# Asking for three z sets and two filter sets in five successive steps

## The chip, the cores and the metric

The kernel runs on one core of one Trainium2 chip. The metric is the device time of one execution in microseconds (us); times below are the median of several executions, and a profile shows one execution.

## The reference

Two blocks follow each other. The first mixes along the sequence with a filter in the frequency domain, the second is a feed-forward layer with a hard-swish:

```
x (8, 3008, 256);  filt_r, filt_i (1505, 256)
X = rfft(x, axis=1);  Y = X * (filt_r + 1j*filt_i);  y = irfft(Y, n=3008, axis=1)
h = y.reshape(24064, 256) @ w_in            # w_in (256, 2048)
g = h * clip(h + 3, 0, 6) / 6
out = g @ w_out                             # w_out (2048, 256)
```

Everything is float32.

## The kernel before

**The transform.** The 3008-point transform of a batch is split as 64 x 47. Its first stage (`a6_unit`, `a6_sums`, L486 to L516) reads x, and GpSimd's queue stores its result as "z" in the DRAM tensor `z_tmp` (`z6_store`, L517). The second stage reads z back, multiplies with 64-point tables on TensorE (`b_unit`, L549), multiplies with the filter on VectorE (`f_unit`, L583 and L584; `y_unit` adds), and transforms back (`bi3_unit`). Its result goes to `g_tmp` in DRAM, from where `t4_load` (L717) fetches it for the last stage (`n_five`, `n_unit`), whose products are the tokens' features `xn`.

**Sets.** A batch's second stage has 12 units, and two units share one z set and one filter set, so there are `NT` = 6 of each per batch, 512 KB apiece. `t2_load(n, c)` (L543) fetches z set c of batch n into one of `TB` = 3 buffers `t2`; `table_load(n, c)` (L257 for batches 2 to 7) fetches filter set c from `f_tmp` into one of `FB` = 2 buffers `ft`. `b_unit(n, 2c)` needs z set c; `f_unit(n, 2c)` needs filter set c.

**The feed-forward layer.** The 24064 tokens are 47 blocks of 512, held as 256 pairs. A block has `NP` = 8 steps, one for each 256 columns of `w_in`; a step takes some 5.6 us when nothing of the transform is in it. The layer uses a Strassen-like scheme with seven products for eight. `up_1` to `up_5` make h in two PSUM tiles `al` and `be`; VectorE adds corrections to them (L835 reads `be`, L840 reads `al`), ScalarE makes the clipped factor (L854), VectorE multiplies (L859). `down` multiplies the result of the step before with `w_out` into four PSUM tiles `po`. `out_1` to `out_5` collect a finished block, and `store` (L988) writes it: one DMA of 256 KB to the DRAM tensor `o_tmp` (L990), seven to ten DMAs of up to 47 rows of 1 KB straight into the output (L993), and, in some blocks, one DMA from `o_tmp` into the output (L998, 423 to 752 KB), for the rows that are mirrored in the sequence.

**Order.** The order of the work is written out by hand. `at(step, fn, ...)` puts a piece of the transform into a step of the feed-forward layer, and a step runs its pieces in places: 3 and 4 at its head (with a `b_unit` and its `f_unit` beside an `n_five`), 0 and 1 in its middle, 2 at its end. All loads are in place 2. Each engine works through its own instructions in that order. All loads and stores named here but `z6_store` and `g3_store` are issued on SyncE's queue, which works in order too.

With k the first step of batch n's tokens, the last piece of the first stage stands in step k-41. The five steps that matter here are called +0 (step k-40) to +4 (step k-36). In the kernel before, +0 ends with five loads. Step +1 is the second step of a block and holds the `store` of the block before (at `out_5`, ahead of place 2). Step +2 has, in places 3 and 4, `n_five`, `b_unit(n, 0)` and `f_unit(n, 0)`. Step +3 has `t4_load` and `f_unit(n, 1)` at its end, and step +6 `b_unit(n, 2)` and `f_unit(n, 2)`. In step +2 the last product into `al` (`up_5`, called A22 below) comes after L840's reading of `al`, which comes after `f_unit(n, 0)` on VectorE.

Of the kernel before, what the change touches and what calls it, by code (L numbers as in the profile page):

```python
# [44 lines left out]
TB = 3  # L45
FB = 2
# [130 lines left out]
def kernel(  # L177
# [498 lines left out]
    for b in range(B):  # L676
# [4 lines left out]
        n = 0  # L681
# [336 lines left out]
    def at(step, fn, *a):  # L1018
        plan.setdefault((step, 0 if fn in EARLY else 1 if fn in (w_scale, bi3_unit, a6_unit) else 2), []).append((fn, a))

    with tc.manual_schedule():
# [175 lines left out]
        def places(n):  # L1197
            if n == 1:
                return (list(range(2, NB + 2)), [12, 13, 14, 18, 19, 20, 22, 23, 26, 27, 29, 31],
                        [13, 15, 16, 19, 21, 22, 24, 25, 28, 30, 30, 32], [17, 24, 30, 34])  # L1200
            k = first[n] * NP
            a_at = [k - 7 * NP + i for i in A_AT]
            f_at, y_at, bi_at = ([k - (5 - 2 * r) * NP + i for r in range(2) for i in p]
                                 for p in ((2, 3, 6, 7, 12, 13), (4, 5, 10, 11, 14, 15), (11, 16)))
            return a_at, f_at, y_at, bi_at
# [4 lines left out]
        for n in range(1, B):  # L1210
            a_at, f_at, y_at, bi_at = places(n)
            for c, s in enumerate(a_at):
                at(s, a_unit if n == 1 else a6_unit, n, c)
                at(s, a_sums if n == 1 else a6_sums, n, c)
                at(s, *((z_store, n, c, nc.sync) if n == 1 else (z6_store, n, c)))
                if c >= (3 if n == 1 else 2):
                    at(max(a_at[c - 3 + (n > 1)], s - 6), x_load, n, c)
                elif n > 1:
                    at(max(prev[-1 if n == 2 else c - 2], s - 6), x_load, n, c)
            for c in range(NT):  # L1220
                s = f_at[2 * (c - TB) + (n == 1)] + 1 if c >= TB else a_at[-1] + 1
                at(s, t2_load, n, c)
                s = f_at[2 * (c - FB) + 1] + 1 if c >= FB else a_at[-1] + 1
                at(s, table_load, n, c)
                if n == 1:
                    at(f_at[2 * c], table_store, c)
            for i in range(NU):
                if (f_at[i], 3) in plan and n > 1:
                    plan[f_at[i], 3].append((b_unit, (n, i)))
                elif i % 2 == 0 or n == 1:  # L1230
                    at(f_at[i], b_unit, n, i)
                if i % 3 == 0:
                    at(bi_at[i // 3], bi3_unit, n, i)
                    at(bi_at[i // 3], g3_store, n, i)
                at(y_at[i], y_unit, n, i)
            for i in range(NU):
                if (f_at[i], 3) in plan and n > 1:
                    plan.setdefault((f_at[i], 4), []).append((f_unit, (n, i)))
                else:
                    at(f_at[i], f_unit, n, i)  # L1240
            prev = a_at
# [122 lines left out]
```

## Time and profile before

| | |
|---|---|
| median of three executions | 2613.17 us (2611.69 to 2617.41) |
| the profiled execution | 2615.35 us, of which the span is 2613.5 |
| TensorE busy | 2588.2 us of the span (99%) |
| VectorE busy | 1894.6 us (72%) |
| ScalarE busy | 1298.1 us (50%) |
| GpSimd busy | 444.1 us (17%) |
| mean granted TensorE clock | 0.997 |
| z set loads (L543) | 42 of 512 KB |
| filter set loads (L257) | 36 of 512 KB |

The span runs from the first to the last instruction that the profile shows. Busy times of different engines overlap. A line "idle ... <-X" names what ended an engine's idle time. For SyncE the profile shows when it issues a DMA and how long the issue takes; when a DMA has landed is taken from the completion marks that the trace keeps for each.

### The profile page before, as it was taken

Reading aid. Unit: us, or ns where it says so; the run is one execution under the profiler, and the core shown is the slowest. Engines: PE = TensorE matmul, PEld = TensorE weight load, DVE = VectorE, ACT = ScalarE, POOL = GpSimd, SP = SyncE. Lnnn points to the kernel's source line nnn. Section 1 sums busy time; section 2 is a strip of 40 time slices with the busy share of each in tenths; the row PEclk is TensorE's granted clock in tenths of the full one; section 3 lists DMA queues with packets and bytes.
Section 4 is the critical chain, followed back from the end, with each engine's and each line's share of the span. In section 5 each row is a group of like instructions: output and inputs, shape, how many; then the busy total and the mean of one; then the engine's idle time right before and its main releaser. Section 6 shows DMA issues by size and latency. Waiting matters only on the chain.

```text
span 2613.5 us, 87737 instructions
## 1 busy us (share of the span) xinstructions
PE 2588.2 (99%) x38466; PEld 2071.5 (79%) x38466; DVE 1894.6 (72%) x3526; ACT 1298.1 (50%) x2682; POOL 444.1 (17%) x671
## 2 busy tenths in 40 slices
PE   8999999999999999999999999999999999999998
PEld 4588877888788887888878888778877888888886
DVE  7877777777777776777777777767776777767665
ACT  4554454545545455454554445545455454555554
POOL 3251031101311012110121101211102111011110
PEclk9999999999999999999999999999999999999999
DMA  9734233222332222321223222232122321111000
GB/s 241 212 110 117 70 103 101 57 57 63 88 106 67 57 61 80 114 63 55 65 73 114 65 61 58 74 111 64 54 61 79 114 64 35 49 44 25 18 22 25
DMA packets 119141, 202.51 MB, mean 77 GB/s; under 512 B 17522, under 2 KB 85712, under 8 KB 118374
## 3 DMA queue, kind: packets, MB, share of 16 engines
q1 hardware_dynamic: 105261, 148.30, 19.9%
q0 software_dynamic: 13216, 48.35, 7.0%
q8 instruction: 302, 4.95, 0.8%
q14 instruction: 81, 0.66, 0.1%
q10 hardware_dynamic: 281, 0.24, 0.0%
HBM read 121.42 MB, written 87.13 MB: 80 GB/s over the span
## 4 chain that ended last, share of the span: by engine, by line
PE 98%; DMA 0%; issue 0%; ACT 0%; DVE 0%; SPq 0%; POOL 0%; POOLq 0%; ACTq 0%
PE po L806 45%; PE al L806 25%; PE be L806 19%; PE psf L565 1%; PE psf L498 1%; PE psn L746 1%; PE al L746 1%; PE psf L640 1%; PE be L640 1%; PE be L498 1%; PE psf L573 0%; DMA g_tmp<-t 0%; PE psf L471 0%; PE psn L806 0%; PE be L746 0%
## 5 line engine op out<-in xcount | busy, mean ns | idle before, releaser
L806 PEld LDWEIGHTS po<-w_all,g 128*64 128x64 f32 x20808 | 1248.0, 137 | 229.0 <-issue 12.7
L806 PE MATMUL po<-w_all,g 128*64 128x128 f32 (+1 forms) x20808 | 1416.4, 274 | 2.6 <-issue 2.6
L854 ACT ACTIVATE r<-h,half_c 128x512 f32<-128x512 f32 x736 | 530.8, 721 | 301.9 <-DVE h L835 290.0
L806 PE MATMUL al<-xt,w_all 128*64 128x256 f32 x4416 | 670.5, 380 | 0.1
L859 DVE SCALAR_TENSOR_TENSOR g<-r,h 128x512 f32<-128x512 f32 x736 | 524.9, 713 | 198.8 <-ACT r L854 196.2
L806 PE MATMUL be<-xt,w_all 128*64 128x256 f32 x2944 | 446.7, 379 | 0.0
L835 DVE TENSOR_TENSOR h<-be,s 128x512 f32<-128x512 f32 x368 | 254.0, 690 | 195.4 <-PE be L806 179.8
L806 PEld LDWEIGHTS be<-xt,w_all 128*64 128x64 f32 x2944 | 215.1, 137 | 104.2 <-issue 0.8
L849 ACT ACTIVATE h<-al 128x256 f32<-128x256 f32 x368 | 141.4, 384 | 302.6 <-PE al L806 301.9
L806 PEld LDWEIGHTS al<-xt,w_all 128*64 128x64 f32 x4416 | 284.3, 137 | 1.5 <-issue 0.7
L840 DVE TENSOR_TENSOR h<-al,s 128x256 f32<-128x256 f32 x368 | 156.3, 425 | 172.8 <-PE al L806 170.4
L867 DVE TENSOR_TENSOR g<-g 128x512 f32<-128x512 f32 x367 | 254.8, 694 | 12.6
L806 PE MATMUL al<-xn,w_all 128*64 128x256 f32 (+1 forms) x1536 | 241.5, 392 | 1.0 <-DVE g L859 0.6
L830 ACT ACTIVATE s<-al 128x256 f32<-128x256 f32 x368 | 141.5, 385 | 195.8 <-PE al L806 195.7
L806 PE MATMUL be<-xn,w_all 128*64 128x256 f32 (+1 forms) x1536 | 238.7, 389 | 0.0
L821 ACT ACTIVATE s<-be 128x256 f32<-128x256 f32 x368 | 141.4, 384 | 173.0 <-PE be L806 173.0
L801 POOL TENSOR_TENSOR xt<-xn 128x256 f32<-128x256 f32 x184 | 140.1, 781 | 355.7 <-ACT xn L726 355.6
L820 ACT ACTIVATE s<-al 128x256 f32<-128x256 f32 x368 | 141.5, 385 | 85.2 <-PE al L806 85.2
L963 POOL TENSOR_TENSOR o<-p,o 128x256 f32<-128x256 f32 x46 | 33.8, 735 | 788.2 <-DVE o L961 788.2
L866 DVE TENSOR_TENSOR g<-g 128x256 f32<-128x256 f32 x367 | 158.5, 432 | 12.6
L806 PEld LDWEIGHTS be<-xn,w_all 128*64 128x64 f32 x1536 | 112.9, 137 | 60.8 <-issue 7.8
L872 DVE TENSOR_TENSOR g<-g 128x256 f32<-128x256 f32 x367 | 156.6, 427 | 3.2
(169 smaller groups left out, 1731.8 us busy)
## 6 DMA issues: line engine op xcount, KB each, us to landing
t<-g_tmp SPq DMA_DIRECT2D x184, 120.0 KB
t<-z_tmp SPq DMA_DIRECT2D x42, 512.0 KB
g_tmp<-t POOLq DMA_DIRECT2D x56, 384.0 KB, 4.9
ft<-f_tmp SPq DMA_DIRECT2D x36, 512.0 KB
z_tmp<-t POOLq DMA_DIRECT2D x120, 144.0 KB, 3.5
o_tmp<-o SPq DMA_DIRECT2D x46, 256.0 KB
xs<-in_x_dram SPq DMA_DIRECT2D x60, 192.0 KB
out_dram<-o SPq DMA_DIRECT2D x165, 47.0 KB
```

The costliest lines, as they stand in the source:

```text
L806: nc.tensor.matmul(ps[ds(o, STRIP)], w[:, ds(o, STRIP)], x, skip_group_check=True, **kw)
L820: nc.scalar.activation(out=s[:, 0, :], in_=al, func=AXT.Copy)
L821: nc.scalar.activation(out=s5, in_=be[:, 1, :], func=AXT.Copy)
L830: nc.scalar.activation(out=s[:, 1, :], in_=al, func=AXT.Copy)
L835: nc.vector.tensor_tensor(out=st["h"][0].rearrange("p (a n) -> p a n", a=2), in0=be, in1=s, op=ALU.add)
L840: nc.vector.tensor_tensor(out=st["h"][1][:, 256:512], in0=al, in1=s5, op=ALU.add)
L849: nc.scalar.activation(out=st["h"][1][:, 0:256], in_=al, func=AXT.Copy)
L854: nc.scalar.activation(out=r, in_=st["h"][i], func=AXT.Relu, bias=half_c, scale=1.0 / 6.0)
L859: nc.vector.scalar_tensor_tensor(out=st["g", k, p][:, o:o + 2, :].rearrange("p a n -> p (a n)"), in0=st["r", i], scalar=1.0, in1=st["h"][i ...
L866: v.tensor_tensor(out=g[:, G1, :], in0=g[:, G3, :], in1=g[:, G22, :], op=ALU.add)
L867: v.tensor_tensor(out=g[:, G3:G2 + 1:2, :], in0=g[:, G3:G1 + 1, :], in1=g[:, G11:G11 + 1, :].broadcast_to([P, 2, 256]), op=ALU.subtract)
L872: nc.vector.tensor_tensor(out=g[:, G4, :], in0=g[:, G12, :], in1=g[:, G2, :], op=ALU.subtract)
```

## The change

For batches 2 to 7 the five loads at the end of step +0 are spread: z set 0 stays in +0, filter set 0 goes to +1, z set 1 to +2, filter set 1 to +3, z set 2 to +4.

```
             for c in range(NT):
-                s = f_at[2 * (c - TB) + (n == 1)] + 1 if c >= TB else a_at[-1] + 1
+                s = f_at[2 * (c - TB) + (n == 1)] + 1 if c >= TB else a_at[-1] + 1 + 2 * c * (n > 1)
                 at(s, t2_load, n, c)
-                s = f_at[2 * (c - FB) + 1] + 1 if c >= FB else a_at[-1] + 1
+                s = f_at[2 * (c - FB) + 1] + 1 if c >= FB else a_at[-1] + 1 + (2 * c + 1) * (n > 1)
                 at(s, table_load, n, c)
```

Here `a_at[-1]` is step k-41. z set 3 (`c >= TB`) stays in step +3 and so now stands ahead of z set 2. On SyncE the built programs differ in nothing but this order, the same in all six batches (batch 2, with L993's DMAs written as one row):

```
before                          after
L543 t2 <- z_tmp   (z set 0)    L543 t2 <- z_tmp   (z set 0)
L257 ft <- f_tmp   (filter 0)   L990 o_tmp <- o
L543 t2 <- z_tmp   (z set 1)    L993 out <- o      x8
L257 ft <- f_tmp   (filter 1)   L998 out <- o_tmp
L543 t2 <- z_tmp   (z set 2)    L257 ft <- f_tmp   (filter 0)
L990 o_tmp <- o                 L543 t2 <- z_tmp   (z set 1)
L993 out <- o      x8           L717 t4 <- g_tmp   x4
L998 out <- o_tmp               L257 ft <- f_tmp   (filter 1)
L717 t4 <- g_tmp   x4           L543 t2 <- z_tmp   (z set 3)
L543 t2 <- z_tmp   (z set 3)    L543 t2 <- z_tmp   (z set 2)
L257 ft <- f_tmp   (filter 2)   L257 ft <- f_tmp   (filter 2)
```

## The prediction

> **What bounds the kernel.** I read the page first, then SyncE's timeline around one batch's second stage, then VectorE's and TensorE's for the same stretch, the windows for the transfers and the clock, and last the order of the built programs.
>
> ```profile
> PE 2588.2 (99%) x38466; PEld 2071.5 (79%) x38466; DVE 1894.6 (72%) x3526; ACT 1298.1 (50%) x2682; POOL 444.1 (17%) x671
> PE 98%; DMA 0%; issue 0%; ACT 0%; DVE 0%; SPq 0%; POOL 0%; POOLq 0%; ACTq 0%
> ```
>
> TensorE works 2588.2 of 2613.5 us. No stage has more than a few us to give back; any wait that reaches TensorE is paid in full. The change adds no instruction; it moves four of the five loads of batches 2 to 7 on SyncE. So the question is whether something TensorE depends on comes too late. SyncE's timeline for batch 3 (start, duration, line):
>
> ```profile
> 733.90 0.38 SPq L543 DMA_DIRECT2D t<-z_tmp  x1
> 734.33 0.46 SPq L257 DMA_DIRECT2D ft<-f_tmp  x1
> 734.84 0.43 SPq L543 DMA_DIRECT2D t<-z_tmp  x1
> 735.31 0.47 SPq L257 DMA_DIRECT2D ft<-f_tmp  x1
> 736.13 0.36 SPq L543 DMA_DIRECT2D t<-z_tmp  x1
> 739.95 0.36 SPq L990 DMA_DIRECT2D o_tmp<-o  x1
> 741.11 8.54 SPq L993 DMA_DIRECT2D out_dram<-o  x9
> 749.70 0.89 SPq L998 DMA_DIRECT2D out_dram<-o_tmp  x1
> ```
>
> All five loads stand ahead of the block's `store`: one copy to `o_tmp`, nine row stores, one copy back. In the changed program filter set 0 stands behind all of these eleven. Its first reader is `f_unit(n, 0)`, in place 4, at the head of VectorE's work in step +2 (L583, L584):
>
> ```profile
> 744.89 0.69 DVE L583 TENSOR_TENSOR s<-psf,ft 128x512 f32<-128x512 f32 x1 [0.20 <-PE psf L565]
> 745.50 0.68 DVE L584 TENSOR_TENSOR s<-psf,ft 128x512 f32<-128x512 f32 x1
> 748.10 0.69 DVE L835 TENSOR_TENSOR h<-be,s 128x512 f32<-128x512 f32 x1 [1.92 <-PE be L806]
> 748.89 0.42 DVE L840 TENSOR_TENSOR h<-al,s 128x256 f32<-128x256 f32 x1
> ```
>
> It runs 3.78 us after the first row store is asked for (741.11), while SyncE is still handing out the row stores. TensorE's next product into `al` (A22, `up_5`) must wait until L840 has read `al`:
>
> ```profile
> 749.55 0.60 PE L806 MATMUL al<-xn,w_all 128*64 128x256 f32 x4
> ```
>
> **When filter set 0 lands.** A row store of 47 rows is slow. In batch 5, where five of the seven have 47 rows (window; busy us of PE, PEld, DVE, ACT, POOL; clock, DMA share, GB/s):
>
> ```profile
> 1386.00:1388.00 2.00, 2.00 (x38) 1.86 (x36) 1.66 (x6) 0.72 (x1) 0.73 (x1) 1.00 1.04 401
> 1394.00:1396.00 2.00, 2.00 (x28) 1.50 (x26) 0.16 (x1) 1.02 (x3) 1.84 (x4) 1.00 0.07 24
> 1400.00:1402.00 2.00, 2.00 (x30) 1.64 (x28) 1.87 (x5) 0.77 (x2) 0.00 (x0) 1.00 0.97 296
> ```
>
> Loads fill all DMA engines (share 1.04, 401 GB/s); the row stores run at a share of 0.07, one engine of sixteen, 24 GB/s. The trace's completion marks say the same: batch 5's 47-row stores land at 1393.80, 1395.79, 1397.79, 1399.79 and 1401.78, 2.0 us apart; the copy back that is next on that queue lands at 1404.53, and what SyncE asked for behind it lands after it, 6 to 8 us after it was asked for. A 512 KB load is spread over all sixteen engines, so its share on the slow one comes last. A filter set in an empty queue lands 3.2 us after issue (asked for at 433.75, landed at 436.92); in a row of loads each adds 1.3 us (414.76, 416.03, 417.33).
>
> I work out the landing per batch from before's own chain of stores: the first 47-row store lands 4.45 us after the first row store is asked for where no load is in the way (469.93 to 474.42, 576.66 to 581.11), 0.5 us more where the first has 17, 19 or 34 rows (0.7 to 0.8 us on that engine); from there to the copy back's landing the spacing is as before; then 1.3 us for filter set 0. In us, batches 2 to 7:
>
> ```
> first row store asked  416.17  741.11  1064.59  1388.09  1713.33  2044.30
> f_unit wants it (+3.78) 419.95 744.89  1068.37  1391.87  1717.11  2048.08
> filter set 0 lands     430.4   758.6   1079.8   1405.1   1730.0   2061.6
> late by                 10.5    13.7     11.4     13.2     12.9     13.5
> TensorE stands           8.3    11.6      9.3     11.1     10.7     11.4
> ```
>
> **What TensorE feels.** VectorE is in order, so L835 and L840 queue behind the waiting L583, and behind them A22. Undisturbed, L840 ends 4.42 us after L583 starts (744.89 to 749.31), of which 1.92 is idle; A22 starts 0.24 later. So 2.15 us is cover, the rest of the lateness is TensorE standing: 62.4 us over six batches.
>
> **The clock.** Before shows one stop of this kind, in batch 6 at `b_unit` (2.91 us, released by nothing the profile names):
>
> ```profile
> 1717.00:1719.00 2.00, 0.00 (x1) 0.00 (x0) 0.00 (x0) 0.06 (x1) 1.86 (x3) 1.00 0.22 65
> 1719.00:1721.00 2.00, 1.09 (x6) 0.28 (x8) 0.00 (x0) 0.00 (x0) 1.84 (x4) 0.58 0.13 39
> 1721.00:1723.00 2.00, 2.00 (x14) 1.52 (x16) 1.29 (x2) 0.08 (x1) 1.24 (x2) 0.50 0.07 24
> ```
>
> The granted clock went to 0.50 and was back at about 1726.15, 6.24 us after TensorE had resumed at 1719.91: 3.1 us lost. Stops three to four times as long should do this each time: 6 x 3.1 = 18.6 us. The bounds are 0 and 3.1 each; I take the upper one, the only row there is. The Trainium skill, "TensorE: Matmul & The Clock Gate", part 1 (the clock gate), has the clock halved after an idle window of about 3.4 us and full again after one busy window of about 3.4 us. By its shortest case a stall would cost an estimated 1.7 us instead, and the sum would be 8.4 us lower; the row disagrees twice, since 2.91 us sufficed and half speed outlasted the stop by 6.24.
>
> **What is given back.** From the first row store to the end of L840 it is 8.20 us in batches 3 and 4, but 9.68, 9.23, 14.73 and 9.72 in 2, 5, 6 and 7: 10.6 us of short TensorE stops labelled "issue", the clock loss above among them, all in or just behind the burst of loads. In the changed kernel the end of that stretch is set by filter set 0's landing, so these stops lie within the new one whatever causes them. I subtract 10.6.
>
> **The other moves cost nothing I can find.** z set 1 and filter set 1 land some 1.3 and 6 us behind filter set 0 (four loads of `t4` between, 3.0 us to ask for); they are wanted at `b_unit` and `f_unit` 2 (770.49 and 775.66 in batch 3, and everything is by then about 11 us later): 10 us or more to spare. z set 2 lands a few us later and is wanted at 809.81. z set 3 is asked for ahead of set 2 and into a buffer free since the batch before; set 2 now waits for `b_unit(n, 0)`, as set 3 did. z set 5 takes set 2's buffer and waits for the same product as before. `store` is only moved up. GpSimd's and ScalarE's queues hold no moved transfer. Without that cover a late z set would cost its lateness directly.
>
> **Sum.** Against the profiled execution's own time, 2615.35 us (span 2613.5, 1.85 around it): +62.4 + 18.6 - 10.6 = +70.4, so 2685.8. That execution lies 2.2 us above the median of three; since the stops that differ between executions lie in the new one's shadow, I keep 2686.
>
> **Rivals.** (1) *Filter set 0 does not queue behind the rows.* If only SyncE's issue delays it, it is asked for about 7.0 us after the first row store (eight row stores take 5.95 us without loads ahead, the copy back 0.9) and lands 3.2 later, at +10.2: 6.4 late, TensorE stands 4.25; 6 x 4.25 + 18.6 - 10.6 = +33.5, 2649. The Trainium skill, "DMA: Bandwidth & Descriptors", section on the anatomy of one DMA, prices a transfer at 2.0 us plus bytes over 436 GB/s, an estimated 3.2 us for 512 KB, which is this case and the empty-queue row. Against: everything behind row stores landed 6 to 8 us after issue. 0.10.
> (2) *Faster.* The burst (2.5 MB at 401 GB/s) is what starves TensorE's instruction stream, and spreading it removes the 10.6 us: 2604.8. It decides only if filter set 0 lands within 3.78 + 2.15 = 5.9 us of the first row store, before SyncE has even finished asking for eight of them. 0.03.
> (3) *No change*: the wait is hidden and the stops stay: 2613 to 2616. 0.02.
> (4) *Worse*: after each stall TensorE meets, at half clock, a further late transfer or a stop like the old ones, some 3.1 us a batch: 2704. 0.08.
> That the change does not do what it says is excluded by the built order: all six batches have the same new order.
>
> **Numbers.** The forecast itself has 0.77. Its own bounds: clock loss from half of 3.1 up (-9), landings a us either way (6), stops returned 8 to 11. The range reaches from rival 1 to rival 4: 2648 to 2704. Slower by over 0.2% (5 us, about what a measurement here can tell) 0.95, within it 0.02, faster 0.03.
>
> **What would show it.** Right: SyncE with filter set 0 behind L998; L583 idle some 10 to 14 us six times on `ft`, released by a DMA; A22 waiting for L840; six stretches at clock 0.50; no "issue" stops left in those steps. Wrong: filter set 0 landing with the row stores (rival 1), L583 idle under 2 us (rivals 2, 3), or the time lost at `b_unit` 2 or `f_unit` 2 instead.

## The result and the profile after

The changed kernel takes 2684.8 us (2684.24 to 2686.34), 1.0274 times the kernel before, 95% interval 1.0259 to 1.0289. Its profiled execution has a span of 2682.5 us against 2613.5, 69.0 more, at a mean granted clock of 0.985.

From the page, engine totals and the shares of the chain that ended last:

```profile
PE 2597.3 (97%) x38466; PEld 2072.5 (77%) x38466; DVE 1892.4 (71%) x3526; ACT 1298.3 (48%) x2682; POOL 443.9 (17%) x671
PE 94%; DMA 3%; SPq 2%; DVE 1%; issue 0%; ACT 0%; POOL 0%; POOLq 0%; DVEq 0%
```

The instruction counts are unchanged. TensorE's busy time grew by 9.1 us only, so 60 of the 69 us are time in which it does nothing, and the chain now holds 3% of DMA and 2% of SyncE's queue, where before it was TensorE alone. The waits (what waited <- for what: us in total, times, longest) name the place:

```profile
DVE s L583 <- DMA ft<-f_tmp: 82.5, 6, 14.8
...
PE al L806 <- DVE h L840: 65.9, 6, 12.0
```

Six times, once for each moved batch, `f_unit(n, 0)` waits for filter set 0, and A22 waits for L840 behind it. For batch 3, SyncE's timeline and then VectorE's:

```profile
752.05 7.88 SPq L993 DMA_DIRECT2D out_dram<-o  x9
759.97 0.90 SPq L998 DMA_DIRECT2D out_dram<-o_tmp  x1
760.91 1.66 SPq L257 DMA_DIRECT2D ft<-f_tmp  x1
762.63 0.42 SPq L543 DMA_DIRECT2D t<-z_tmp  x1
```

```profile
754.93 0.69 DVE L867 TENSOR_TENSOR g<-g 128x512 f32<-128x512 f32 x1
770.43 0.69 DVE L583 TENSOR_TENSOR s<-psf,ft 128x512 f32<-128x512 f32 x1 [14.81 <-DMA ft<-f_tmp]
771.03 0.68 DVE L584 TENSOR_TENSOR s<-psf,ft 128x512 f32<-128x512 f32 x1
771.63 0.68 DVE L835 TENSOR_TENSOR h<-be,s 128x512 f32<-128x512 f32 x1
772.23 0.41 DVE L840 TENSOR_TENSOR h<-al,s 128x256 f32<-128x256 f32 x1
```

Filter set 0 is asked for 8.86 us after the first row store and lands 9.42 us later, at 770.34 by its completion mark; L583 starts 0.09 us after that. VectorE's four instructions then run without a gap, and A22 starts at 772.70, where the bracket gives TensorE's idle time before it:

```profile
772.70 0.69 PE L806 MATMUL al<-xn,w_all 128*64 128x256 f32 x2 [12.04 <-DVE h L840]
```

In the windows (busy us of PE, PEld, DVE, ACT, POOL; clock, DMA share, GB/s) no engine does anything in the first stretch, while the DMA engines are busy:

```profile
764.00:766.00 2.00, 0.00 (x0) 0.00 (x0) 0.00 (x0) 0.00 (x0) 0.00 (x0) 0.50 0.98 284
772.00:774.00 2.00, 1.30 (x8) 0.93 (x10) 1.67 (x4) 0.85 (x2) 0.00 (x0) 0.50 1.05 265
776.00:778.00 2.00, 2.00 (x20) 1.33 (x18) 1.31 (x3) 0.76 (x2) 0.00 (x0) 0.77 0.20 77
```

The clock is at 0.50 in the stand and for 4.22 us after it (from the trace's record of the clock). All six batches, in us after the first row store is asked for (the last two rows are durations):

```
batch                     2      3      4      5      6      7
filter set 0 asked       6.24   8.86   7.73   8.57   8.72   9.22
last row store lands    10.87  13.88  11.87  13.65  13.28  13.79
copy back lands         12.85  15.87  13.42  15.73  15.37  15.61
filter set 0 lands      15.86  18.28  15.35  18.23  17.63  18.02
TensorE stands           9.62  12.04   9.11  11.99  11.39  11.78   sum 65.9
0.50 after the stand     3.94   4.22   3.87   4.23   4.83   3.97   half of it 12.5
```

### The profile page after: what moved, and what is told of

Same layout as the page of the kernel before. It is cut to its first block, busy times and chain, and to the rows that moved or that the text cites. A ratio compares the mean times of both kernels' runs of the same rounds, so it can differ in the third digit from the quotient of the medians.

```text
span 2682.5 us, 87730 instructions
## 1 busy us (share of the span) xinstructions
PE 2597.3 (97%) x38466; PEld 2072.5 (77%) x38466; DVE 1892.4 (71%) x3526; ACT 1298.3 (48%) x2682; POOL 443.9 (17%) x671
## 4 chain that ended last, share of the span: by engine, by line
PE 94%; DMA 3%; SPq 2%; DVE 1%; issue 0%; ACT 0%; POOL 0%; POOLq 0%; DVEq 0%
PE po L806 43%; PE al L806 24%; PE be L806 18%; DMA ft<-f_tmp 2%; SPq L993 1%; PE psf L498 1%; PE psf L565 1%; PE psn L746 1%; PE psf L640 1%; PE be L640 1%; PE al L746 1%; PE be L498 1%; PE psf L573 0%; DMA g_tmp<-t 0%; PE psf L471 0%
## 5 line engine op out<-in xcount | busy, mean ns | idle before, releaser
L806 PEld LDWEIGHTS po<-w_all,g 128*64 128x64 f32 x20808 | 1248.6, 137 | 229.9 <-issue 10.3
L806 PE MATMUL al<-xn,w_all 128*64 128x256 f32 (+1 forms) x1536 | 244.0, 397 | 66.9 <-DVE h L840 65.9
L840 DVE TENSOR_TENSOR h<-al,s 128x256 f32<-128x256 f32 x368 | 156.1, 424 | 171.6 <-PE al L806 169.7
L806 PEld LDWEIGHTS al<-xn,w_all 128*64 128x64 f32 x1536 | 94.6, 138 | 99.8 <-DVE h L840 67.4
L866 DVE TENSOR_TENSOR g<-g 128x256 f32<-128x256 f32 x367 | 158.5, 432 | 12.6
```

The costliest lines, as they stand in the source:

```text
L806: nc.tensor.matmul(ps[ds(o, STRIP)], w[:, ds(o, STRIP)], x, skip_group_check=True, **kw)
L840: nc.vector.tensor_tensor(out=st["h"][1][:, 256:512], in0=al, in1=s5, op=ALU.add)
L866: v.tensor_tensor(out=g[:, G1, :], in0=g[:, G3, :], in1=g[:, G22, :], op=ALU.add)
```

## Experiments

Each was compared with the kernel before on the same chip, where that took 2613.0 to 2613.6 us.

### Where the time comes from

**f0_back**: the changed kernel with filter set 0 back in +0.

```
-  ... else a_at[-1] + 1 + (2 * c + 1) * (n > 1)
+  ... else a_at[-1] + 1 + (2 * c + 1) * (n > 1) * (c > 0)
```

> The changed kernel with filter set 0 alone put back into step +0, ahead of the store; the other three loads stay spread. Theory A (the whole loss is filter set 0 behind the row stores on the one busy DMA engine): no wait of L583 on ft, no clock loss, and the time is that of the kernel before less up to 10.6 us of short TensorE stops: 2602 to 2616 us. Theory B (SyncE's issue time alone delays filter set 0): the same. Theory C (the spread as such costs, through z set 1, filter set 1 or z set 2 coming late): still 2640 us or more, with waits at units 2 to 4.

Measured: 2606.21 us, ratio 0.9976 (0.9967 to 0.9985). The waits hold no row for `ft<-f_tmp`. The other three moved loads cost nothing, and this kernel is faster than both others, by 0.24% than the kernel before. The stretch from the first row store to the end of L840, whose excess over 8.20 us adds up to 10.6 us in the kernel before, has an excess of 0.4 us here: the short stops are gone, even with filter set 0 in its old place.

**f0_only**: the kernel before with filter set 0 alone moved to +1.

```
-  ... else a_at[-1] + 1                  # table_load
+  ... else a_at[-1] + 1 + (n > 1) * (c == 0)
```

> The kernel before with filter set 0 alone moved behind the store; z sets 1 and 2 and filter set 1 stay ahead of it. Theory A: the whole loss, and some us more than the changed kernel, since three more loads ahead hold the row stores up by 0 to 3 us a batch: 2682 to 2700 us. Theory B: 2680 to 2690 us. Theory C: near the kernel before, 2613 us.

Measured: 2690.48 us, ratio 1.0298 (1.0284 to 1.0312), clock 0.985, the wait on `ft` 85.8 us in six pieces. The one move makes the whole loss. It is 5.7 us worse than the full change. The two z sets and filter set 1 that stay in +0 push the queue back (filter set 0 lands 16.6 to 19.0 us after the first row store against 15.4 to 18.3), but by the profiled executions that lengthens TensorE's stands only from 65.9 to 67.4 us in all. The half clock after them costs 15.8 us against 12.5, and an "issue" stop of 1.29 us is left in batch 6.

**z2_only**: the kernel before with z set 2 alone, the fifth load of the burst, moved behind the store, to +4.

```
-  ... else a_at[-1] + 1                  # t2_load
+  ... else a_at[-1] + 1 + 4 * (n > 1) * (c == 2)
```

> The kernel before with z set 2 alone moved behind the store, into step +4; four loads stay together instead of five. If the short TensorE stops in and behind the burst come from the length of the burst (five loads, 6.4 us at 400 GB/s): part of the 7 us that the run with only z set 0 and filter set 0 ahead of the store gained, 2607 to 2611 us. If they come from anything else in those steps: 2613 us, within 1 us.

Measured: 2606.44 us, ratio 0.998 (0.9971 to 0.9989), the gain of f0_back with one load, and a little more than was expected. On SyncE (batch 3), four loads are left in the burst, and z set 2 is now the second of the pair at 753.40:

```profile
735.49 0.47 SPq L257 DMA_DIRECT2D ft<-f_tmp  x1
740.14 0.36 SPq L990 DMA_DIRECT2D o_tmp<-o  x1
741.30 7.66 SPq L993 DMA_DIRECT2D out_dram<-o  x9
749.01 1.05 SPq L998 DMA_DIRECT2D out_dram<-o_tmp  x1
750.18 3.18 SPq L717 DMA_DIRECT2D t<-g_tmp  x4
753.40 1.49 SPq L543 DMA_DIRECT2D t<-z_tmp  x2
```

The stretch's excess is 1.1 us instead of 10.6. So the "issue" stops go with the burst's fifth load. By what they are tied to it can be read from the trace of the kernel before, where TensorE stops for 1.26, 0.42, 2.91 and 1.20 us in batches 2, 5, 6 and 7. They make up most of these two rows of its waits, and their sum of 5.8 us, the 3.1 us of half clock in batch 6 and what follows from them make the 10.6:

```profile
PE po L806 <- issue: 3.7, 4, 1.3
PE psf L565 <- issue: 3.3, 2, 2.9
```

The page's DMA queue q8, named `instruction`, brings 302 packets of 16 KB. TensorE has 76,932 products and weight loads, some 255 for each packet, so by this count the packets are TensorE's instructions. Each of the four stops ends 1.4 to 1.5 us after such a packet has landed, the 43rd, the 159th, the 198th and the 237th; and TensorE goes on with 195 or 196 records of its trace more than 43, 159, 198 and 237 times 256 behind it, the same place in a packet's worth each time. So TensorE waited there for its instructions, as rival 2 had it. The four packets take 0.9 to 1.0 us each but start late: the 198th starts 4.2 us after the first row store, against 1.7 us here and 1.1 in f0_back. Why the burst makes them start late (by the DMA engines that both use, perhaps) is not shown, and the fifth load is not all of it: behind packet 198, in batch 6, TensorE still stops for 0.47 us here and for 1.38 us in f0_first below, where one load alone is left in +0.

### Why filter set 0 is so late

**split_rows**: the changed kernel, with the row stores of these six stores cut, where they are longer than 16 rows, into a multiple of 16 and a rest.

```
-  nc.sync.dma_start(raw(out, ..., [[NC * D, m], [1, D]]), o[p:p + m, h, u, :])
+  cut = m - m % 16 if k + 6 in first[2:] and m > 16 and m % 16 else m
+  for q, w in ((0, cut), (cut, m - cut)):
+      if w:
+          nc.sync.dma_start(raw(out, ..., [[NC * D, w], [1, D]]), o[p + q:p + q + w, h, u, :])
```

> The changed kernel, but in the six stores that stand ahead of filter set 0 each row store of more than 16 rows is cut into a multiple of 16 rows and a rest, so that no long one runs on one DMA engine; SyncE has 14 to 17 row stores to ask for instead of 7 to 10. Theory A: the stores land about as fast as they are asked for, filter set 0 lands 3 to 4 us after it is asked for, about 10.5 us after the first row store; late by 6.7, TensorE stands 4.3 us a batch; with the clock some 2640 us (2628 to 2655). Theory B: filter set 0 is asked for no earlier and lands 8 to 10 us after that as in the changed kernel: 2680 us or more.

Measured: 2670.74 us, ratio 1.0222 (1.0208 to 1.0236): between the two numbers, a miss for both. Most pieces now land some 1.5 us after they are asked for, and the last lands 7.9 to 10.0 us after the first is asked for, so the queue on one engine is gone. But two things that neither theory priced were behind it. Asking for 14 to 17 pieces takes 7.0 to 9.0 us, no less than asking for the seven to ten whole ones (5.3 to 8.2):

```profile
751.74 8.68 SPq L996 DMA_DIRECT2D out_dram<-o  x17
760.46 0.88 SPq L1001 DMA_DIRECT2D out_dram<-o_tmp  x1
761.39 0.59 SPq L257 DMA_DIRECT2D ft<-f_tmp  x1
```

and the copy back, with no more than 1.1 us of row stores still to land ahead of it, itself lands 4.7 to 5.1 us after it is asked for; filter set 0 lands 1.3 to 1.7 us behind it.

**f0_rows**: filter set 0 asked for after the row stores and ahead of the copy back, and no longer in its place of the changed kernel.

```
+          if k + 6 in first[2:]:            # after the row stores, ahead of L998
+              table_load(first.index(k + 6), 0)
```

> The changed kernel with filter set 0 asked for between the row stores and the copy back (it still waits for all rows, but no longer for the copy back). Queue theory: it lands 1.4 us behind the last row store instead of 1.4 behind the copy back, about 14.3 us after the first row store instead of 17.2; TensorE stands some 8 us a batch instead of 11; 2668 us (2662 to 2673). Issue theory: it is asked for 0.94 us earlier a batch and gains no more than that: 2679 us.

Measured: 2667.13 us, ratio 1.0205 (1.0188 to 1.0222), on the queue's number. Filter set 0 lands 0.8 to 1.8 us after the last row store and 5.9 to 7.8 us after it is asked for. The waits:

```profile
DVE s L583 <- DMA ft<-f_tmp: 64.0, 6, 12.2
...
PE al L806 <- DVE h L840: 46.7, 6, 9.4
```

**split_f0_rows**: both edits, split rows and filter set 0 ahead of the copy back.

> The kernel with cut row stores, and filter set 0 asked for between them and the copy back. If the copy back's own transfer (4 to 5 us there) is what still held filter set 0 in the run with cut rows, then now only SyncE's issue of the rows is ahead of it: asked for at about +8.2 us, landing 3.3 later at +11.5, TensorE stands 5.3 us a batch; 2653 us (2646 to 2659). If the copy back's transfer doesn't matter: 2665 us, the 0.9 us of its issue a batch.

Measured: 2650.81 us, ratio 1.0139 (1.0124 to 1.0155), on the first number. Filter set 0 now lands 3.2 to 4.0 us after it is asked for, which is an empty queue's time (3.1 to 4.0 us for the filter sets of the kernel before that found all earlier DMAs of SyncE landed). The stand is what SyncE's asking leaves:

```profile
DVE s L583 <- DMA ft<-f_tmp: 46.4, 6, 8.8
...
PE al L806 <- DVE h L840: 29.4, 6, 6.0
```

**f0_first**: filter set 0 right behind the copy to `o_tmp` (L990), ahead of all row stores, still in +1; the same two lines as in f0_rows, placed before the row stores.

> The changed kernel with filter set 0 asked for right behind the copy to o_tmp, one place behind the head of the store, ahead of all row stores. Queue theory: it lands about 3.5 us after that, about 1 us or more before f_unit wants it; no wait on ft, as with filter set 0 in step +0: 2602 to 2612 us. If what counts is that it stands behind any part of the store, or the step it is put in: 2640 us or more.

Measured: 2608.06 us, ratio 0.9976 (0.9967 to 0.9985). No wait on `ft<-f_tmp` is left. Batch 3, SyncE and then VectorE:

```profile
739.31 0.38 SPq L990 DMA_DIRECT2D o_tmp<-o  x1
739.73 0.47 SPq L257 DMA_DIRECT2D ft<-f_tmp  x1
740.63 8.48 SPq L995 DMA_DIRECT2D out_dram<-o  x9
```

```profile
744.25 0.69 DVE L583 TENSOR_TENSOR s<-psf,ft 128x512 f32<-128x512 f32 x1 [0.20 <-PE psf L565]
```

It lands at 743.26, 0.99 us before it is read. Step +1 itself isn't too late, then; the place behind the row stores is.

**f0_pool**: the changed kernel with filter set 0 on GpSimd's queue, in +1.

```
-  nc.sync.dma_start(ft[...], f_d[c])
+  (nc.sync if c else nc.gpsimd).dma_start(ft[...], f_d[c])
```

> The changed kernel with filter set 0 asked for in step +1 as there, but on GpSimd's queue, where nothing of the store stands ahead of it. Theory A: it is asked for right after L963, about 1 us ahead of the first row store, and lands about 5 us later, near the time when f_unit wants it; L583 waits at most 2 us, and the time is 2602 to 2622 us. Theory B: the same, since SyncE no longer delays it. Theory C: 2640 us or more.

Measured: 2610.65 us, ratio 0.9989 (0.998 to 0.9998), no wait on `ft<-f_tmp`. Another queue removes the loss as another place does. It gives 2.4 us where f0_back gives 6.8. The six stretches have no excess here (0.05 us); but in its profiled execution TensorE stops for 1.72 us at 30.0 us, on the load `wi<-wi_t`, and has 3.41 us of half clock behind that, as no other profiled execution has. That is 3.4 of the 4.2 us between the two profiled executions; whether it belongs to the change is not known.

The four places in the queue part the loss. Of the 71.6 us between the changed kernel and 2613.2, 17.7 go with the copy back (2684.8 to 2667.1), 16.3 with the rows' one-engine queue (to 2650.8), and 42.7 with the asking for row stores on SyncE (to 2608.1); that last state lies 5 us below the kernel before. The parts depend on the order of the steps: with the rows cut first (split_rows), the rows have 14.1 and the copy back 19.9. The last two are parted less sharply than it looks, since the split itself adds issues. TensorE's stands in the four profiled executions are 65.9, 46.7, 29.4 and none, and the half clock after them costs 12.5, 12.0, 16.1 and nothing.

### The clock

**warm**: the changed kernel with products of a zero tile, added to a bank of `po`, put ahead of A22 in +2 to keep TensorE busy while it would stand. They add nothing to the result.

```
+  none = const.tile([P, P], FP32, name="none")              # memset to 0
+  if p == 2 and k + 5 in first[2:]:
+    for r in range((83, 106, 78, 105, 99, 103)[first.index(k + 5) - 2]):
+        strips(st["po", kd][0][:, 0, r % 2, :], none, w_out[pd][:, B11, :], start=False, stop=False)
```

> The changed kernel with TensorE kept busy while it stands: ahead of A22 in step +2 of the six batches, 83, 106, 78, 105, 99 and 103 pairs of products with a zero tile are added into a po bank (they add nothing), about 0.6 us less a batch than the stand measured in the changed kernel. If the half clock after each stand costs what its records say (about 12.5 us in all): clock at 1.0 throughout and 2672 us (2668 to 2677). If the half clock costs nothing that counts, because VectorE or the transfers set the pace after the stand: 2685 us, within 2 us.

Measured: 2729.56 us, ratio 1.0444 (1.0428 to 1.0459). A miss of size: a call left four records where I had reckoned with two. The group of the added products:

```profile
L807 PE MATMUL po<-w_all,none 128*64 128x128 f32 x2296 | 126.7, 273 | 0.6 <-issue 0.6
```

126.7 us of products in stands of 65.9 push everything back; the run says nothing about the clock's price.

**warm_half**: half as many (41, 53, 39, 52, 49, 51).

> As the run with zero products, with half as many: 41, 53, 39, 52, 49 and 51 pairs. There each pair left four records of 55 ns apart instead of the two reckoned with, so the products lasted 125 us in all instead of 63, and covered twice the stand. Now they last about 62.5 us against stands of 65.9. If the half clock after each stand costs what its records say (12.5 us in all): clock at 1.0 throughout, and 2672 us (2669 to 2676). If it costs nothing: 2685 us.

Measured: 2674.88 us, ratio 1.0235 (1.0221 to 1.0249). The products take 63.2 us, the clock stays at 1.00, and filter set 0 is as late as in the changed kernel:

```profile
764.00:766.00 2.00, 2.00 (x41) 2.00 (x39) 0.00 (x0) 0.00 (x0) 0.00 (x0) 1.00 1.06 309
772.00:774.00 2.00, 1.54 (x26) 1.15 (x24) 1.87 (x5) 0.72 (x1) 0.00 (x0) 1.00 1.00 257
```

```profile
DVE s L584 <- DMA ft<-f_tmp: 83.0, 6, 15.0
...
PE al L807 <- DVE h L841: 4.2, 6, 1.0
```

The same stand without the clock's fall is 9.9 us cheaper than the changed kernel. The two intervals leave that uncertain by some 5 us, which holds the 12.5 reckoned from the windows and not the 18.6 of the prediction.

## Why the prediction was right, and where it was not

**The mechanism was right.** Filter set 0 behind L998, six waits on `ft`, A22 behind L840 and six stretches at 0.50 are all there. f0_only shows that this one load makes the loss; f0_back shows that z set 1, filter set 1 and z set 2 cost nothing where they went.

**When filter set 0 lands** was mis-sized, low by about 5.5 us over the six batches. The term was the last one, 1.3 us behind the copy back, taken from loads in a row. It measured 1.9 to 3.0, mean 2.4. The copy alone doesn't make that: in split_rows, where no slow row stands ahead of the copy, filter set 0 lands 1.3 to 1.7 us behind it. What makes the rest stays open. The cover was 2.4 to 2.5 instead of 2.15, because VectorE's four instructions close up. So the stand was 65.9 us against 62.4 (+3.5).

**The clock** was mis-sized the other way: 2.1 us a batch, 12.5 in all, against 3.1 and 18.6 (-6.1). The step that failed was to take the upper bound because it was the only row. That row had 6.24 us at half speed after a stop; the six new stops, three to four times as long, had 3.9 to 4.8. In all, the clock was at 0.50 for 10.24 us in two batches and 13.65 in four: three and four times 3.413. The Trainium skill, "TensorE: Matmul & The Clock Gate", part 1 (the HAM clock gate), has a free-running window of 3413 ns and full speed after one busy window. The trace agrees with the window's length; what followed a stop was 0.5 to 1.4 us more than one window. Its shortest case, an estimated 10.2 us in all, was nearer to the measured 12.5 than the forecast's 18.6. On when the clock falls the trace still asks less: in batch 3 it fell about 2.6 us into the stand (TensorE stops at 760.66, and the window from 762 to 764 has 0.82), as before it fell with a stop of 2.91. Nor is the price of a stop fixed: in split_f0_rows, with stops of 4.3 to 6.0 us, the clock was at 0.50 for 6.83 us each time, 4.7 to 6.0 us of that after the stop, and the loss was 16.1 us, more than in the changed kernel; in f0_rows it was 12.0, in split_rows 14.6, in f0_only 15.8.

**What is given back** was right in size, 10.6 us, for the execution that the sum starts from: f0_back's profiled span is 10.3 us below that of the kernel before. Its median is only 6.8 below. Batch 6's half clock, 3.1 of the 10.6, seems to be in few executions only: that execution's mean clock is 0.997, and of the 49 that the experiments were compared with four have 0.997 or less. The prediction left the cause open. z2_only ties the stops to the fifth load of the burst, and the packets of the `instruction` queue to TensorE's late instructions, which makes half of rival 2 true: the stops do go when the burst shrinks, but the gain shows only in a version that doesn't make filter set 0 late.

**Sum.** 65.9 + 12.5 - 10.6 = 67.8, and the span grew by 69.0. The forecast's +70.4 is close because its two errors cancel (+3.5 and -6.1); by terms it was right to some 6 us and not to 1.

**Rival 1** fell: filter set 0 landed 7.6 to 9.7 us after it was asked for, not 3.2. (The row that the 3.2 was read from, 433.75 to 436.92, had a z set still ahead that landed at 434.93, but truly empty queues gave 3.1 to 4.0; and the Trainium skill's formula that is set beside it there is a fit for DMAs asked for by GpSimd, where this load is SyncE's.) Its two parts can be seen by themselves, though. With nothing slow ahead (split_f0_rows) it lands in 3.2 to 4.0 us and the time is 2650.8, 1.8 us from the rival's 2649; the rival's stands and clock, 25.5 and 18.6, measured 29.4 and 16.1. The Trainium skill, "DMA: Bandwidth & Descriptors", has the number of DMA engines chosen as the largest one up to 16 that divides the outermost size (section on why a DMA increments its semaphore by 16): by that 47 rows go to one engine and 16 or 32 rows to sixteen. The trace agrees: besides a mark at its asking a 47-row store has one completion mark, a piece of 16 or 32 rows has sixteen; and the first 47-row store of a batch lands 4.0 to 4.6 us after it is asked for, the pieces 1.5 us after (median). **Rival 4** found nothing: the waits show no further stop after the stand. **Rivals 2 and 3** needed a landing within 5.9 us of the first row store; it came at 15.4 or later.

## What to carry to other kernels

Putting a load into a later step of a kernel with an in-order queue doesn't delay it by that step, it puts it behind whatever that queue is asked for in between; price the slowest transfer there, on the one DMA engine that carries it, and the time of asking. Spread a burst by moving only the loads with slack: here the fifth load alone brings 0.2% (z2_only), the first needed load alone costs 3% (f0_only). A wait of an in-order engine costs TensorE its length less a small cover, 2.5 us here, and half clock on top, which took 1.5 to 3.0 us a stop in these runs.

## What the runs showed of the hardware that was not expected

- A row of 47-row stores makes SyncE itself slow. In batch 3 the last three row stores take 1.73, 1.96 and 1.88 us to ask for, against 0.26 to 0.41 for the first ones, while the stores land 2.0 us apart.
- The copy back lands 4.7 to 5.1 us after it is asked for with next to nothing ahead (split_rows), but only some 2 us after the last row store when it has queued behind one.
- A TensorE stop that the waits label "issue" was a wait for instructions: in the kernel before, the four stops in these stretches end 1.4 to 1.5 us after a 16 KB packet of the queue `instruction` lands.
